# Decode attention: keys and probabilities transposed on VectorE, scores of four heads in one matmul

## The chip, the cores and the metric

One core of one Trainium2 chip runs the whole program. The metric is the device time of one launch in microseconds (us). TensorE is called PE, VectorE DVE, ScalarE ACT, GpSimd POOL and the queue of SyncE SP. A difference under 0.2% (0.4 us) counts here as no difference.

## The reference, cut to what matters

```python
xn = layernorm(x)                                   # x: [8, 1, 512], bf16
q  = (xn @ wq) -> [8 batches, 32 heads, 128]        # wq: [512, 4096]
k, v = caches[:, :, 8192 - 2048:, :]                # [8, 8 kv heads, 2048, 128] are read
s  = einsum(q, repeat(k, 4)) * 128 ** -0.5          # four query heads share one kv head
o  = softmax(s) @ repeat(v, 4)                      # per batch: 32 heads x 128
attn = o.reshape(8, 1, 4096) @ wo                   # wo: [4096, 512]
glu  = (sigmoid(xn @ w_gate) * (xn @ w_up)) @ w_down   # F = 1792
out  = x + attn * silu(glu)
```

With eight rows of x the arithmetic is small. What is large is the data: 64 MiB of keys and values in the window and 13 MiB of weights are read once.

## The kernel before

**Transfers.** All large transfers are issued on SP's queue into nine slots of SBUF (16 KB a partition each). `pump` issues the next transfer of a list in a fixed order as soon as `free` returns a slot. The list is: the gate, up and down weights, the query weights `wq`, then the key tiles and value tiles of the eight batches in turn (a tile is 2 MiB: one batch, four kv heads, 2048 positions), the value tile three places behind the key tile, and last `wo` in four pieces of 16, 10, 4 and 2 rows a partition. The key tiles are numbered k0 to k15 here and the value tiles v0 to v15 (two a batch); k15 is thus followed by v12, v13, v14, v15 and the four pieces of `wo`, wo16, wo10, wo4 and wo2.

`w_down` has 1792 rows, 14 x 128. The first 11 x 128 come as one transfer over all partitions, 11 KB each (`want_down`, `MT = 11`). The rest comes in eight small transfers (`want_side`): four of 5, 5, 3 and 3 partitions with 15 KB each, four of 9 partitions with 4 KB each.

**Per batch.** A key tile has its positions on the partitions and must be turned, since the contraction of the scores is over the 128 values of a head. `k_transposes` does it on PE: 8 transposes of 128x128 into a PSUM tile `kT_ps`, which DVE copies to `kT_sb` (line 461), 16 such steps a batch. `scores` then runs four matmuls a pair of steps, one for each kv head l, side by side in the four column groups of the array, each with 32 columns of weights (line 474); all scores of a batch end in one PSUM bank of 128 rows, where a row is one query head and one quarter of its positions, and the 512 columns are those positions:

```python
nc.tensor.matmul(
    s_ps[b][NR * l : NR * (l + 1), :],
    lhsT=qm_sb[:, b, i * G + l, o : o + Z],
    rhs=t[:, :, PG * l : PG * (l + 1)],
```

`row_max` takes the maximum of each row on DVE (line 487) and four exponentials on ACT (line 494, 32 rows each). The maxima and sums of the rows of one head are brought to one value by `stat_rows`, `factor` and `spread` on one partition. `p_transposes` turns the probabilities on PE (line 563) and DVE copies them to `pT_sb` (line 568). `value` multiplies them with the value tile (line 584): for the batches under `WIDE = 5` one matmul a kv-head group with 64 columns of weights and 512 moving columns, from batch 5 on two with 32 and 256. `combine` (ACT, line 604), `normalise` (PE and DVE, lines 614 and 623) and `turn` (lines 632 and 639) put the batch's outputs into `oP_sb`.

**Order.** Each engine runs in the order in which the program was written; the scheduler is off. In batch b's 16 steps PE also does the softmax work of batch b-1 and the values of batch b-2. After the loop the last two batches are finished, and `fin_ps` takes 32 x 4 matmuls of 128 columns over `wo` (line 706); two DVE operations (lines 717 and 719) and four small output transfers end the program.

## Time and profile before

| | |
|---|---|
| median of 3 runs | 199.16 us (199.14 to 199.21) |
| the profiled execution's own time | 199.33 us |
| its span, first to last instruction | 197.5 us |
| mean granted PE clock | 0.965 |
| read from memory | 81.01 MB |
| PE busy | 157.4 us, 2112 matmuls |
| DVE busy | 125.4 us, 245 instructions |
| ACT busy | 40.7 us |
| POOL busy | 11.0 us |

Busy time is what an engine spent in instructions. Matmuls overlap in the array, so PE's figure is an upper one. 1.83 us of the profiled execution's own time lie outside its span. In the rows of groups, `x128 | 84.2, 683` means 128 instructions, 84.2 us busy, 683 ns each. The time in which an engine was idle before them, and what ended it, stands behind the next bar.

### The profile page before, as it was taken

What the parts mean: (1) busy time and instruction counts of PE and PEld (TensorE: products, weight loads), DVE (VectorE), ACT (ScalarE), POOL (GpSimd) and SP (SyncE); (2) the same over time, 40 slices, a digit from 0 to 9 for tenths busy, and PEclk for the clock granted to TensorE, in tenths of its full rate; (3) what the DMA queues carried; (4) which work ended last, traced back from release to release, by engine and by line L of the source; (5) the groups of instructions that cost most, each with busy time, mean ns of one, the idle gap of its engine ahead of it and who ended that gap; (6) DMA issues with size and microseconds to landing.
All of it is one profiled execution on the core that took longest, in us unless ns stands there. A gap on an engine that the chain in (4) does not pass through costs nothing.

```text
span 197.5 us, 4796 instructions
## 1 busy us (share of the span) xinstructions
PE 157.4 (80%) x2112; PEld 103.1 (52%) x2112; DVE 125.4 (63%) x245; ACT 40.7 (21%) x95; POOL 11.0 (6%) x22
## 2 busy tenths in 40 slices
PE   0089559999788898799979987999799979976733
PEld 0034325776664565466545654566466556655531
DVE  4623106999797696679666965796669658935201
ACT  0522022006306001600160016001600160071000
POOL 8910200000000000000000000000000000000000
PEclk9999859999999999999999999999999999999975
DMA  6999999999999999999999999999999999999980
GB/s 205 424 440 435 431 434 435 425 425 431 423 425 425 438 428 435 431 425 428 422 433 431 435 425 433 428 418 428 428 438 431 428 428 431 428 423 425 428 366 21
DMA packets 6396, 81.32 MB, mean 412 GB/s; under 512 B 812, under 2 KB 820, under 8 KB 1624
## 3 DMA queue, kind: packets, MB, share of 16 engines
q1 hardware_dynamic: 6328, 81.01, 96.6%
q8 instruction: 16, 0.26, 0.5%
q10 hardware_dynamic: 48, 0.01, 0.0%
q14 instruction: 4, 0.03, 0.0%
HBM read 81.01 MB, written 0.01 MB: 410 GB/s over the span
## 4 chain that ended last, share of the span: by engine, by line
DMA 73%; PE 22%; POOL 3%; SPq 0%; issue 0%; DVE 0%; POOLq 0%
DMA v_sb<-in_A_v_cache_dram 46%; DMA wo_sb<-in_A_wo_dram 14%; PE kT_ps L456 11%; DMA wq_sb<-in_A_wq_dram 7%; DMA k_sb<-in_A_k_cache_dram 6%; PE o_ps L584 4%; PE s_ps L474 3%; POOL side L126 2%; PE m_ps L614 1%; PE fin_ps L706 1%; PE pT_ps L563 1%; SPq L131 0%; POOL perm L206 0%; POOL hT_sb L245 0%; DVE prod L717 0%
## 5 line engine op out<-in xcount | busy, mean ns | idle before, releaser
L461 DVE COPY kT_sb<-kT_ps 128x1024 bf16<-128x1024 bf16 x128 | 84.2, 683 | 28.9 <-PE kT_ps L456 25.0
L456 PE MATMUL kT_ps<-perm,k_sb 128*128 128x128 bf16 x1024 | 72.6, 220 | 3.7 <-DMA k_sb<-in_A_k_cache_dram 3.7
L456 PEld LDWEIGHTS <-k_sb 128*128 128x128 bf16 x1024 | 58.8, 98 | 26.1 <-issue 16.8
L584 PE MATMUL o_ps<-v_sb,pT_sb 128*32 128x256 bf16 (+1 forms) x352 | 36.5, 327 | 9.0 <-DMA v_sb<-in_A_v_cache_dram 7.6
L474 PE MATMUL s_ps<-kT_sb,qm_sb 128*32 128x512 bf16 x256 | 25.6, 389 | 1.3 <-DVE kT_sb L461 1.1
L494 ACT ACTIVATE p_buf<-s_ps,st 32x512 bf16<-32x512 f32 x32 | 21.7, 679 | 15.4 <-DVE st L487 15.1
L584 PEld LDWEIGHTS <-pT_sb 128*32 128x32 bf16 (+1 forms) x352 | 12.3, 101 | 21.7 <-issue 19.7
L604 ACT ACTIVATE o_sb<-o_ps,fac 128x512 f32<-128x512 f32 (+1 forms) x8 | 4.9, 608 | 60.9 <-PE o_ps L584 60.9
L568 DVE COPY pT_sb<-pT_ps 128x1024 bf16<-128x1024 bf16 x16 | 10.8, 676 | 1.8 <-PE pT_ps L563 1.8
L474 PEld LDWEIGHTS <-qm_sb 128*32 128x32 bf16 x256 | 7.0, 93 | 8.0 <-issue 1.3
L563 PE MATMUL pT_ps<-turn_rows,p_buf 128*128 128x128 bf16 x128 | 10.7, 227 | 0.0
L563 PEld LDWEIGHTS <-p_buf 128*128 128x128 bf16 x128 | 9.4, 149 | 0.2 <-issue 0.2
L521 ACT ACTIVATE w_row<-w 1x128 f32<-1x128 f32 x8 | 2.5, 309 | 30.6 <-DVE w L514 30.6
L235 PE MATMUL xnT_ps<-ident,xn_bf 8*128 8x8 bf16 x4 | 0.3, 176 | 10.6 <-DVE xn_bf L224 10.6
L385 DVE COPY qm_sb<-qT_ps 128x128 bf16<-128x128 bf16 x2 | 1.4, 881 | 8.7 <-PE qT_ps L380 8.7
L301 DVE TENSOR_TENSOR h_bf<-sig,u_ps 8x448 bf16<-8x448 f32 x4 | 2.4, 608 | 6.6 <-PE u_ps L294 6.1
L278 PE MATMUL g_ps<-wg_sb,xnT_sb 128*8 128x448 bf16 x16 | 5.7, 544 | 0.3 <-DVE xnT_sb L242 0.3
L494 ACT ACTIVATION_READ_ACCUMULATOR p_buf<-s_ps,st 32x1 f32 x32 | 5.9, 184 | 0.0
L706 PE MATMUL fin_ps<-wo_sb,oP_sb 128*32 128x128 bf16 x128 | 3.3, 263 | 3.1 <-DMA wo_sb<-in_A_wo_dram 3.1
L487 DVE TENSOR_REDUCE st<-s_ps 128x1 f32<-128x512 f32 x8 | 5.4, 681 | 0.5 <-PE s_ps L474 0.5
L235 PEld LDWEIGHTS <-xn_bf 8*128 8x128 bf16 x4 | 0.2, 117 | 10.6 <-DVE xn_bf L224 10.6
L352 PE MATMUL q_ps<-wq_sb,xnT_sb 128*32 128x512 bf16 x32 | 3.1, 526 | 3.2 <-DMA wq_sb<-in_A_wq_dram 3.2
(88 smaller groups left out, 92.0 us busy)
## 6 DMA issues: line engine op xcount, KB each, us to landing
k_sb<-in_A_k_cache_dram SPq DMA_DIRECT2D x16, 2048.0 KB
v_sb<-in_A_v_cache_dram SPq DMA_DIRECT2D x16, 2048.0 KB
wq_sb<-in_A_wq_dram SPq DMA_DIRECT2D x2, 2048.0 KB
wo_sb<-in_A_wo_dram SPq DMA_DIRECT2D x1, 2048.0 KB
wg_sb<-in_B_w_gate_dram SPq DMA_DIRECT2D x2, 896.0 KB
wu_sb<-in_B_w_up_dram SPq DMA_DIRECT2D x2, 896.0 KB
wd_sb<-in_B_w_down_dram SPq DMA_DIRECT2D x1, 1408.0 KB
wo_sb<-in_A_wo_dram SPq DMA_DIRECT2D x1, 1280.0 KB
```

The costliest lines, as they stand in the source:

```text
L126: nc.gpsimd.memzero(t[:M_AT])
L278: nc.tensor.matmul(g_ps[:], lhsT=xnT_sb[:, kt, :B], rhs=weights[("wg_sb", kt)][:, k * FC : (k + 1) * FC], start=(kt == 0), stop=(kt == KT ...
L456: nc.tensor.transpose(out=kT_ps[:, c, :], in_=k_sb[:, j * CU + h * CH + c, :], identity=perm[:],)
L461: nc.vector.tensor_copy(out=kT[(b, u)][:, h * CH : (h + 1) * CH, :], in_=kT_ps[:])
L474: nc.tensor.matmul(s_ps[b][NR * l : NR * (l + 1), :], lhsT=qm_sb[:, b, i * G + l, o : o + Z], rhs=t[:, :, PG * l : PG * (l + 1)], start=(u ...
L487: nc.vector.tensor_reduce(out=st[b][:], in_=s_ps[b][:], axis=AX.X, op=ALU.max, negate=True)
L494: nc.scalar.activation(out=p_buf[b % 2][rows, :, l, :], in_=s[rows, :].rearrange("k (c p) -> k p c", p=PG), func=AF.Exp, bias=st[b][rows, ...
L563: nc.tensor.transpose(out=pT_ps[:, c, :], in_=p_buf[b % 2][:, :, :, h * CH + c].rearrange("k p l -> k (p l)"), identity=turn_rows[:],)
L568: nc.vector.tensor_copy(out=pT[b][:, h * CH : (h + 1) * CH, :], in_=pT_ps[:])
L584: nc.tensor.matmul(o_ps[r] if b < WIDE else o_ps[r, 0:2], lhsT=pT[b][:, c, r], rhs=x, start=(c == 0), stop=(c == CU - 1), tile_position=(0 ...
L604: nc.scalar.activation(out=o[:, :n], in_=o_ps[:, :n], func=AF.Copy, scale=fac.pop(b)[:])
L706: nc.tensor.matmul(fin_ps[Z * j : Z * (j + 1), :], lhsT=oP_sb[:, t, :], rhs=weights[("wo_sb", t)][:, j * P : (j + 1) * P], start=(t == 0), ...
```

## The change

Keys are no longer turned by PE. DVE transposes each quarter of a key tile in place, in blocks of 32x32, as 32-bit words: a word is a pair of neighbouring bf16 values, and stays a pair. In a key tile a group of 32 partitions holds 8 positions of each of the four kv heads. After the transpose a partition of the group holds one pair of head dimensions, and the 32 words along it are the group's 8 positions of four heads. The contraction over the 128 values of a head is then four matmuls (two halves of the 64 pairs, two members of a pair), and one matmul over all 128 partitions serves the four groups at once: the query weights are laid out (`widen`, on POOL, four copies a batch) so that a column is nonzero only on its own group's 32 partitions. The moving operand is read with a step of two bf16 values.

A row of the scores is a query head and a group's positions, but its 512 columns hold the positions of all four kv heads. A first matmul (`of_row`, `other`) puts -1e30 into the columns of the three other kv heads, so that their exponentials are zero. A batch has four banks of scores instead of one, so the exponentials are four of 128 rows by 512 rather than four of 32 rows by 512, and the row maximum is taken four times.

The maximum is taken over all rows of a head before the exponentials (`both_max`, `head_max`, with two small PE transposes), so the four parts of a head have the same bias and one sum; `stat_rows` and `spread` go. The probabilities are turned by one DVE transpose of pairs a batch (`p_turn`). All batches use the wide form of `value`.

The steps are 8 a batch instead of 16, the values of batch b-2 lie in its last four. The PSUM pool of the transposes goes and the pool of the scores has six banks. The query projection uses all 128 columns of weights (32 matmuls as before, one after another instead of four at a time). `want_down` brings 13 x 128 rows, 13 KB a partition, and the eight side transfers bring the rest in pieces of 5, 5, 5, 5, 3, 3, 3 and 3 partitions of 4 KB. At the end, the first 16 rows of `wo` are multiplied in 16 matmuls of 512 columns into `f_ps`, copied by ACT, and added to `fin_ps` by `fold` ahead of row 26.

```diff
-    LOW, SF = (5, 5, 3, 3), 15
-    MID, SM = 9, 4
-    MT = 11
+    LOW, SF = (5, 5, 3, 3), 4
+    MT = 13
...
-    def k_transposes(b, u, h):
...
+    def k_turn(b, s):
+        i, j = s // NJ, s % NJ
+        x = (
+            k_tiles[(b, i)][0][:, j * CU : (j + 1) * CU, :]
+            .rearrange("p c d -> p (c d)")
+            .bitcast(f32)
+        )
+        nc.vector.transpose(out=x, in_=x)
+
+    def scores(b, s):
+        i, j = s // NJ, s % NJ
+        if j % 2 == 0:
+            s_ps[(b, s // 2)] = ps_s.tile([P, CU, Z], f32, name="s_ps", tag="s")
+            nc.tensor.matmul(
+                s_ps[(b, s // 2)][:],
+                lhsT=of_row[:].rearrange("k y l r -> k (y l r)"),
+                rhs=other[:],
+                start=True,
+                stop=False,
+            )
+        k = k_tiles[(b, i)][0][:, j * CU : (j + 1) * CU, :].rearrange(
+            "p c (x k e) -> p x e c k", x=2, e=2
+        )
+        for n in range(NE):
+            o = (i * NE + n) * P + M0 - NL * (j % 2)
+            nc.tensor.matmul(
+                s_ps[(b, s // 2)][:],
+                lhsT=q_wide[b % 2][:, o : o + P],
+                rhs=k[:, n // 2, n % 2],
+                start=False,
+                stop=(j % 2 == 1 and n == NE - 1),
+            )
+        if j == NJ - 1:
+            free(k_tiles.pop((b, i)))
...
+    def p_turn(b):
+        pT[b] = ppool.tile([P, NBK, CU // 2, Z, 2], bf16, name="pT_sb")
+        nc.vector.transpose(
+            out=pT[b][:].rearrange("p m c x e -> p (m c x e)").bitcast(f32),
+            in_=p_buf.pop(b)[:].rearrange("k m c x e -> k (m c x e)").bitcast(f32),
+        )
...
+        for s in range(1, NS):
+            tasks[s].append(lambda s=s: scores(b, s - 1))
+        for m in range(NBK - 1):
+            tasks[2 * m + 3].append(lambda m=m: row_max(b, m))
         if b >= 1:
+            tasks[0].append(lambda: scores(b - 1, NS - 1))
+            tasks[0].append(lambda: row_max(b - 1, NBK - 1))
+            tasks[0].append(lambda: both_max(b - 1))
+            tasks[1].append(lambda: head_max(b - 1))
+            tasks[2].append(lambda: exps(b - 1))
+            tasks[6].append(lambda: p_turn(b - 1))
+            tasks[6].append(lambda: factor(b - 1))
+        if b + 1 < B:
+            tasks[3].append(lambda: widen(b + 1))
+        if b >= 2:
+            for s in range(NJ, NS):
+                n = (s - NJ) * NN // NJ
+                tasks[s].append(lambda n=n: values(b - 2, n, n + NN // NJ))
+        if b >= 3:
+            tasks[0].append(lambda: combine(b - 3))
+            tasks[3].append(lambda: normalise(b - 3))
+            tasks[5].append(lambda: turn(b - 3))
+        for s in range(NS):
+            k_turn(b, s)
+            for f in tasks[s]:
+                f()
...
     fin_ps = ps_s.tile([P, P], f32, name="fin_ps", tag="s")
-    for t in range(RT):
+    RG = 16
+    f_ps = ps_s.tile([P, D], f32, name="f_ps", tag="s")
+    for t in range(RG):
...
+    f_sb = ktpool.tile([P, D], f32, name="f_sb", tag="kT")
+    nc.scalar.copy(out=f_sb[:], in_=f_ps[:])
+    for t in range(RG, RT):
+        if t == 26:
+            fold(fin_ps, f_sb, False, False)
```

The instruction lists of the two programs, put side by side, have 4091 entries on PE before and 1504 after, 152 and 175 on DVE, 39 and 28 on ACT, 27 and 37 on POOL.

## Prediction

> **What bounds the kernel now.** I read first the slices of the page, then the batches in the middle, then the end.

> ```profile
> PE 157.4 (80%) x2112; PEld 103.1 (52%) x2112; DVE 125.4 (63%) x245; ACT 40.7 (21%) x95; POOL 11.0 (6%) x22
> PEclk9999859999999999999999999999999999999975
> DMA  6999999999999999999999999999999999999980
> q8 instruction: 16, 0.26, 0.5%
> ```

> The transfers are busy from the second slice to the 38th. The stretch of one batch (start and length, busy time of PE, its weight loads, DVE, ACT and POOL, granted clock, DMA share, GB/s):

> ```profile
> 84.00:103.50 19.50, 17.92 (x222) 11.45 (x220) 14.26 (x29) 4.08 (x10) 0.00 (x0) 1.00 1.01 430
> ```

> Four tiles of 2 MiB at 430 GB/s take 19.5 us. PE needs 17.9 of them, DVE 14.3. No engine decides in the middle; the time is the bytes and the two ends. The end, from the timeline (start, length) and by windows:

> ```profile
> 188.81 1.08 PE L706 MATMUL fin_ps<-wo_sb,oP_sb 128*32 128x128 bf16 x64 [1.12 <-DMA wo_sb<-in_A_wo_dram]
> 191.86 2.28 PE L706 MATMUL fin_ps<-wo_sb,oP_sb 128*32 128x128 bf16 x64 [1.97 <-DMA wo_sb<-in_A_wo_dram]
> 194.19 0.29 DVE L717 TENSOR_TENSOR prod<-gg_sb,fin_ps 128x128 f32<-128x128 f32 x1 [6.16 <-PE fin_ps L706]
> ...
> 190.00:191.50 1.50, 0.00 (x0) 0.00 (x0) 0.00 (x0) 0.00 (x0) 0.00 (x0) 0.59 0.78 321
> 191.50:193.00 1.50, 1.14 (x40) 1.06 (x40) 0.00 (x0) 0.00 (x0) 0.00 (x0) 0.50 0.68 265
> 193.00:194.50 1.50, 1.12 (x31) 0.56 (x23) 0.29 (x1) 0.00 (x0) 0.00 (x0) 0.50 0.02 8
> ```

> PE waits for `wo` twice; its last eight matmuls start at 193.74, 0.38 us after the last packet of `wo` (193.36). So the last transfer sets the end. But the DMA share falls to 0.78 and 0.68 before that: the 16 DMA engines do not end together. I followed the trace's packets engine by engine. A 16 KB packet takes 607 ns (37.9 ns a KB) and the next follows at once; after 3 us an engine pauses only where a packet of a program (q8) comes between, at 0.91 us. Three engines carry all four 15 KB rows and four 4 KB rows of the side transfers, 76 KB; two carry 46 KB, four 16 KB, seven none: a side transfer of n partitions uses the same first n engines. The three heavy ones meet no packet of q8 and end at about 193.0 to 193.37. A light one that meets none ends at 190.1; the rest lie between, by how many of the 16 they got.

> **The change, part by part.**

> *Transfers.* The heavy three carried 11 x 8 + 76 = 164 KB of `w_down`, after the change 13 x 8 + 32 = 136 KB: 28 x 37.9 ns = 1.06 us less. The light ones carry 104 KB for 88, 0.61 us more, 190.7. q8's 16 packets of 16 KB over PE's 4091 entries are 64 bytes an entry, so q8 is PE's program; 1504 entries are 6 packets. A light engine with one ends at 191.6, with two at 192.5. So the last packet comes at about 192.3 for 193.36, and all `wo` and late cache tiles about 1.06 us earlier for the heavy engines.

> *DVE.* The 144 copies of `kT_sb` and `pT_sb` (683 and 676 ns) go, 72 transposes of 128x1024 words come. No row shows one. Two reductions of 32-bit words give the scale: 128 words in 0.271 us (line 510) and 512 in 0.681 (line 487), so 1.068 ns a word and 0.134 fixed. For 1024 words that is 1.23 us. Lower bound 0.67, at which two copies of 1024 elements followed each other; upper bound 2.32, two such steps a word. I take 1.23, since these are the rows on 32-bit data. [...] A batch on DVE is then 9 x 1.23 + 4 x 0.68 (maxima) + 2.2 (nine small operations at 0.14 to 0.29) = 16.0 of 19.5 us.

> *PE.* The 1024 key transposes and 128 of probabilities go. A batch has 32 score matmuls and 4 for the mask, one after another. The nearest row is `u_ps`, 448 columns at 3.19 / 16 = 0.199 us, so 0.228 for 512: 8.2 us. A moving step of two is not in any row; bounds 0.228 and double, I take 0.228 because PE's weight loads from `p_buf` (step 32 bytes) lost only half (149 for 98 ns). Values: 16 pairs at 0.275 (line 584, two concurrent), 4.4. With `normalise` 0.65 and small ones 14.1 us. POOL's `widen` is four copies of 32x128, 0.3 each by line 206's 0.42 for 128x128, hidden: due one batch later.

> *Slots.* A key tile is held until its last scores instead of its last PE transpose, some 2 us longer. At the start the query is late: 16 matmuls one after another, 3.65 for 1.90, then POOL's copies, so first scores near 37 instead of 34.5 us and k0's slot near 40. The transfer that takes this slot is k6, eight tiles (39 us) behind k0: covered by 30 us. Cost nothing; if it were not covered, each us would count.

> *The end.* Here cover is thin. k15 is visible to PE at 164.50, so at 163.44 then. DVE: four key transposes and `p_turn(6)` 6.15, one maximum 0.68, `oP` 0.29, `factor` 0.69, a wait for `turn` 0.3: 171.55. Last scores 0.91, maximum 0.68, then `both_max`, `head_max` and the bias, six steps of 0.14 to 0.27 with PE between, 1.42: 174.56. Exponentials 4 x 0.785 (line 494, start to start): 177.7. `p_turn` 1.23: 178.93, by when the one bank `o_ps` is free too (values of batch 6 on PE to 178.3, `combine` 0.69). Values of batch 7: 32 x 0.228 one after another, since a half has its own columns, `normalise(6)` 0.65, `turn` 0.2: 187.1 (v15 is there at 182.85). `combine` to `oP_sb` took 2.2, now with 512 columns 2.4; with 0.3 for PE's own end it is 189.8. Against 188.08 before. Then 16 wide matmuls 1.33 (four at 0.33, line 474): 191.15; rows 16 to 25 0.68; the copy to `f_sb` 0.59 runs beside them; `fold` 0.43 (line 337) to 192.3, rows 26 to 29 0.27 to 192.6; the last two rows wait for wo2, visible at 192.68, plus 0.45: 193.13 for 194.19, a gain of 1.06. But the cover is 0.1 us, over 30 us of handoffs between three engines. I give 0.4 to handoffs that pass it and take 0.65.

> Sum: 199.33 - 0.65 = 198.68 as a profiled execution. Its own time was 0.17 above the median, so 198.5 for the median. Bounds in this case: 198.1 (cover holds) and 198.75.

> **The rivals.** *PE's clock falls at the end (slower).* In the trace the clock is 0.50 from 190.3 on, after a stretch of 3.4 us in which PE was busy 1.5 (186.9 to 190.3); at 0.50 the last 64 matmuls took 2.28 us, for 1.08 at 1.00. The changed kernel is emptier: PE works 14.1 of 19.5 us, waits about 2 us before each key tile, and is nearly idle for 2.4 us between the last value and `oP_sb`. At 0.50 the last part is 1.90 (16 wide, as `q_ps` took at 0.50) + 1.43 + 0.86 + 0.86 + 0.35 = 5.4 us from 189.8: 195.2, 1.0 later than before, 200.2; had the clock fallen before k15 too, some 0.5 to 1 more. It decides once such a stretch holds less than about half PE work. For: the trace's own fall at 1.5 of 3.4. Against: windows with 2.1 of 3.4 stayed at 1.00 (46.9 to 50.3). [...]

> *Cover lost, nothing gained.* The handoffs cost 0.7 to 1.4 us instead of 0.4, or another engine ends last (two packets of q8 on one, 192.5, or on a heavy one, 193.2): 198.8 to 199.5. For: 32 value matmuls in a row and six small steps hang on one chain.

> *The transpose needs twice as long a word.* Then 9 x 2.32 + 4.9 = 25.8 us a batch on DVE exceed 19.5: 33 before k0, 8 x 25.8 and 25 for the end, about 264 us. From 1.62 us each DVE sets the pace. Against: the two reductions' 1.07 ns a word.

> **How the numbers follow.** Cover case 0.47 (faster), lost cover 0.20 (same), clock 0.28 and slow transpose 0.05 (slower). Under 0.4 us, 0.2%, a measurement of this kernel can't be told from no change. The range 198.0 to 200.6 takes in the first three but for a clock that falls twice; the likeliest case alone is 198.0 to 198.75.

> **What would show it.** Transposes at 1.23 us; DMA share at 1.0 to about 190 and a last `wo` packet near 192.3; q8 with 6 packets; `oP_sb` near 190, PEclk 1.00 in 189 to 193. Wrong: transposes over 1.6 us, PE waiting for DVE while DMA share falls in the middle, `fin_ps` ending over 0.6 us after the last packet, or a PEclk of 0.50 before it.

## The result, and the profile after

| | before | after |
|---|---|---|
| median | 199.2 us (199.09 to 199.29, 11 runs) | 201.16 us (199.67 to 205.88, 11 runs) |
| ratio of after to before | | 1.0082 (1.006 to 1.0105) |
| the profiled execution's own time, its span | 199.33, 197.5 | 199.67, 197.9 |
| mean granted clock of the profiled execution | 0.965 | 0.897 |

The kernel is slower by 0.8%, and its executions lie 6 us apart where those of before lay within 0.2. All ratios here leave out executions that are over 1.5% above the fastest of their kernel; of after's eleven these are three, of 203.56 us and more. The profiled execution of after is the shortest of the eleven: what it shows is the changed kernel at its best, and the other 1.5 us of the median have to be looked for in other executions. First its page (busy time; granted clock and DMA share in 40 slices; the queue of PE's program):

```profile
PE 157.5 (80%) x845; PEld 63.2 (32%) x846; DVE 125.7 (64%) x201; ACT 36.9 (19%) x86; POOL 17.0 (9%) x59
PEclk9999699589997579999955999998599879999999
DMA  6999999999999999999999999999999999999970
q8 instruction: 6, 0.10, 0.2%
```

The DMA share is as full as before, and q8 has its 6 packets. New is the clock: before the change it was at 0.50 from 23.0 to 29.8 us and from 190.3 on, and here it is at 0.50 in six stretches before the end, of 3.4 to 10.2 us each. The groups of the turned keys, their scores and the turned probabilities (count, busy time, mean ns of one):

```profile
L449 DVE STREAM_TRANSPOSE k_sb<-k_sb 128x1024 f32<-128x1024 f32 x64 | 77.4, 1225 | 5.5 <-DMA k_sb<-in_A_k_cache_dram 5.5
L467 PE MATMUL s_ps<-k_sb,q_wide 128*128 128x512 bf16 x256 | 77.3, 433 | 4.5 <-DVE k_sb L449 3.9
L530 DVE STREAM_TRANSPOSE pT_sb<-p_buf 128x1024 f32<-128x1024 f32 x8 | 9.6, 1203 | 0.0
```

A transpose takes 1.225 us. The 433 ns of a score matmul is the time of overlapping ones counted whole; the timelines below show four in 1.03 us. Then the stretch of one batch and the three stretches of the end, as before (PE, its weight loads, DVE, ACT, POOL, clock, DMA share, GB/s), and the end's timeline:

```profile
84.00:103.50 19.50, 17.00 (x85) 6.45 (x85) 15.92 (x24) 6.13 (x17) 1.15 (x4) 0.89 1.01 429
190.00:191.50 1.50, 1.08 (x9) 0.98 (x9) 0.29 (x1) 0.00 (x0) 0.00 (x0) 1.00 0.80 325
191.50:193.00 1.50, 1.11 (x21) 0.58 (x25) 0.30 (x1) 0.00 (x0) 0.00 (x0) 1.00 0.35 135
193.00:194.50 1.50, 1.37 (x76) 1.09 (x68) 0.00 (x0) 0.58 (x1) 0.00 (x0) 1.00 0.00 0
```

```profile
164.15 2.37 DVE L449 STREAM_TRANSPOSE k_sb<-k_sb 128x1024 f32<-128x1024 f32 x2 [1.16 <-DMA k_sb<-in_A_k_cache_dram]
...
176.39 2.78 PE L558 MATMUL o_ps<-v_sb,pT_sb 128*64 128x512 bf16 x24
...
177.20 0.69 ACT L520 ACTIVATE p_buf<-s_ps,bias 128x512 bf16<-128x512 f32 x1
...
179.28 0.69 ACT L582 ACTIVATE o_sb<-o_ps,fac 128x512 f32<-128x512 f32 x1 [1.30 <-PE o_ps L558]
179.33 0.30 DVE L615 CAST oP_sb<-m_ps 128x32 bf16<-128x32 f32 x1 [2.54 <-PE m_ps L608]
179.44 1.25 DVE L530 STREAM_TRANSPOSE pT_sb<-p_buf 128x1024 f32<-128x1024 f32 x1
...
180.74 1.91 PE L558 MATMUL o_ps<-v_sb,pT_sb 128*64 128x512 bf16 x8 [0.61 <-DVE pT_sb L530]
...
182.59 1.08 PE L590 MATMUL m_ps<-ident_f,o_sb 128*128 128x32 f32 x8
...
191.72 0.30 DVE L615 CAST oP_sb<-l_ps 128x32 bf16<-128x32 f32 x1 [0.28 <-PE l_ps L608]
...
192.07 1.05 PE L681 MATMUL f_ps<-wo_sb,oP_sb 128*32 128x512 bf16 x16 [0.39 <-DVE oP_sb L615]
...
194.62 0.29 DVE L707 TENSOR_TENSOR prod<-gg_sb,fin_ps 128x128 f32<-128x128 f32 x1 [2.60 <-PE fin_ps L696]
```

The end no longer waits for `wo` at all. Its last packet is there at 192.94; `f_ps` starts at 192.07 because DVE's last copy to `oP_sb` ends then, and everything behind it waits for that. The chain from k15 (line 449, the first that waits for a DMA) through the last batch has become the bound.

### The profile page after: what moved, and what is told of

It is laid out like the page before. It is cut to its first block, busy times and chain, and to the rows that moved or that the text cites. A ratio compares the mean times of both kernels' runs of the same rounds, so it can differ in the third digit from the quotient of the medians.

```text
span 197.9 us, 2228 instructions
## 1 busy us (share of the span) xinstructions
PE 157.5 (80%) x845; PEld 63.2 (32%) x846; DVE 125.7 (64%) x201; ACT 36.9 (19%) x86; POOL 17.0 (9%) x59
## 4 chain that ended last, share of the span: by engine, by line
DMA 43%; PE 35%; DVE 16%; POOL 2%; ACT 1%; issue 1%; SPq 1%; DVEq 0%; ACTq 0%
DMA k_sb<-in_A_k_cache_dram 31%; PE s_ps L467 15%; PE o_ps L558 12%; DVE k_sb L449 9%; DMA wq_sb<-in_A_wq_dram 7%; DMA wu_sb<-in_B_w_up_dram 5%; DVE st L482 3%; PE s_ps L455 2%; PE m_ps L590 1%; PE q_ps L336 1%; DVE pT_sb L530 1%; POOL qc L367 1%; SPq L99 1%; PE l_ps L590 1%; PE f_ps L681 1%
## 5 line engine op out<-in xcount | busy, mean ns | idle before, releaser
L449 DVE STREAM_TRANSPOSE k_sb<-k_sb 128x1024 f32<-128x1024 f32 x64 | 77.4, 1225 | 5.5 <-DMA k_sb<-in_A_k_cache_dram 5.5
L467 PE MATMUL s_ps<-k_sb,q_wide 128*128 128x512 bf16 x256 | 77.3, 433 | 4.5 <-DVE k_sb L449 3.9
L558 PE MATMUL o_ps<-v_sb,pT_sb 128*64 128x512 bf16 x256 | 38.0, 395 | 0.6 <-DVE pT_sb L530 0.6
L467 PEld LDWEIGHTS <-q_wide 128*128 128x128 bf16 x256 | 22.8, 105 | 39.4 <-issue 24.5
L520 ACT ACTIVATE p_buf<-s_ps,bias 128x512 bf16<-128x512 f32 x32 | 21.5, 686 | 56.4 <-DVE bias L516 56.4
L482 DVE TENSOR_REDUCE st<-s_ps 128x1 f32<-128x512 f32 x32 | 21.4, 669 | 4.6 <-PE s_ps L467 4.4
L558 PEld LDWEIGHTS <-pT_sb 128*64 128x64 bf16 x256 | 13.9, 112 | 18.7 <-issue 9.4
L375 POOL COPY q_wide<-qc 32x128 bf16<-32x128 bf16 x32 | 9.2, 287 | 90.9 <-PE s_ps L467 89.4
L455 PE MATMUL s_ps<-other,of_row 4*128 4x512 bf16 x32 | 14.1, 440 | 2.7 <-POOL of_row L411 2.7
L494 PE MATMUL m_ps<-ident_f,top 128*2 128x128 f32 x8 | 2.4, 296 | 14.3 <-DVE top L491 14.3
L530 DVE STREAM_TRANSPOSE pT_sb<-p_buf 128x1024 f32<-128x1024 f32 x8 | 9.6, 1203 | 0.0
```

Of the source, the lines that this page charges most:

```text
L375: nc.gpsimd.tensor_copy(out=q_wide[b % 2][g, : NW * P].rearrange("p (x c) -> p x c", x=NW)[:, :, M0 + Z * a : M0 + Z * a + NL], in_=qc[g, ...
L449: nc.vector.transpose(out=x, in_=x)
L455: nc.tensor.matmul(s_ps[(b, s // 2)][:], lhsT=of_row[:].rearrange("k y l r -> k (y l r)"), rhs=other[:], start=True, stop=False,)
L467: nc.tensor.matmul(s_ps[(b, s // 2)][:], lhsT=q_wide[b % 2][:, o : o + P], rhs=k[:, n // 2, n % 2], start=False, stop=(j % 2 == 1 and n == ...
L482: nc.vector.tensor_reduce(out=st[b][:, m // 2, m % 2 : m % 2 + 1], in_=s_ps[(b, m)][:].rearrange("k c x -> k (c x)"), axis=AX.X, op=ALU.max,)
L520: nc.scalar.activation(out=p_buf[b][:, m], in_=s_ps.pop((b, m))[:].rearrange("k (c e) x -> k c x e", e=2), func=AF.Exp, bias=bias[:, m // ...
```

## The experiments

The median of before on the chips of the experiments was 199.17, 199.23, 199.22, 199.2 and 199.09 us in the five sets of runs; each ratio is against the runs beside it.

**after_again**: the changed kernel once more, for a second profile.

> The changed kernel once more, for a second profile. Theory 1 (PE's clock): the changed kernel leaves PE idle for some 2 us before each key tile, the granted clock drops to 0.50 for stretches whose place differs from execution to execution, and where such a stretch lies after 150 us the last batch ends later: 199.7 to 206, and the profile has an oP_sb copy of the last batch later than 192.0 if a 0.50 stretch lies between 150 and 195 us. Theory 2 (the chain alone): the last batch's chain of handoffs is late by a fixed 0.4 to 2 us, with all stages stretched alike, whatever the clock shows. Theory 3 (memory): the spread comes from slower transfers; then the last wo packet lies later than 193 in a slow profile.

200.4 us (199.22 to 203.23, 10 runs), ratio 1.0057 (1.0023 to 1.0091). Its profile is of an execution of 203.23 us, the kind that the first profile lacked. Batch 7's scores over k14 and what follows:

```profile
158.30 1.89 PE L467 MATMUL s_ps<-k_sb,q_wide 128*128 128x512 bf16 x4
...
160.66 1.89 PE L467 MATMUL s_ps<-k_sb,q_wide 128*128 128x512 bf16 x4
...
163.91 1.89 PE L467 MATMUL s_ps<-k_sb,q_wide 128*128 128x512 bf16 x4
...
170.21 1.03 PE L467 MATMUL s_ps<-k_sb,q_wide 128*128 128x512 bf16 x4
170.40 0.30 DVE L615 CAST oP_sb<-m_ps 128x32 bf16<-128x32 f32 x1 [3.10 <-PE m_ps L608]
...
173.21 1.23 DVE L449 STREAM_TRANSPOSE k_sb<-k_sb 128x1024 f32<-128x1024 f32 x1
...
194.50 0.30 DVE L615 CAST oP_sb<-l_ps 128x32 bf16<-128x32 f32 x1 [0.28 <-PE l_ps L608]
...
194.85 1.16 PE L681 MATMUL f_ps<-wo_sb,oP_sb 128*32 128x512 bf16 x16 [0.39 <-DVE oP_sb L615]
...
198.18 0.29 DVE L707 TENSOR_TENSOR prod<-gg_sb,fin_ps 128x128 f32<-128x128 f32 x1 [3.39 <-PE fin_ps L696]
```

The clock was 0.50 from 158.1 to 168.4, so four score matmuls took 1.89 us instead of 1.03. The last two key transposes stand on DVE behind the copy of 170.40, and that copy waited 3.10 us for the late PE (0.53 in after). The last key transpose ended at 174.44 for 171.66, and the last copy to `oP_sb` started 2.78 us later. The clock fell again at 195.7, and from the start of `f_ps` to `prod` it took 3.33 us for 2.55: together the 3.56 us by which `prod` is later. The last packet of `wo` came at 193.64, long before it was needed.

**warm**: six 512-column matmuls that feed nothing, at the start and in the middle of each batch.

```diff
+            if s == NJ:
+                keep_warm(b, s // 2)
...
+            tasks[0].append(lambda: keep_warm(b, 0))
```

> Six extra matmuls of 512 columns twice a batch, in the places where PE otherwise waits for a key tile; results overwritten by the mask matmul. Theory 1: granted clock 0.95 or more, spread of the runs under 0.6 us, median 199.5 to 200.0 (what is left is the fixed late end of 0.4). Theory 2 and 3: median near 201 and the same spread, since 2.6 us more PE work a batch helps neither a chain nor memory.

200.34 us (199.31 to 203.62, 5 runs), ratio 1.0064 (1.0044 to 1.0084): a miss. The mean clock rose only to 0.937 to 0.964, and an execution of 203.62 was among the five. The profiled one (199.31) had no fall between 128.4 and 196.6, and so no group of 1.89 in batch 7; even then `prod` started at 194.24.

**early**: `p_turn(last)` stands ahead of `turn(last - 2)`, so that DVE turns the last probabilities before it waits for PE's values.

```diff
-    turn(last - 2)
     combine(last - 1)
     p_turn(last)
+    turn(last - 2)
```

> Only the order of the last batch: p_turn stands ahead of turn of batch 5 in DVE's order. In the profile of the changed kernel p_turn starts at 179.44 though the exponentials end at 177.97, behind the copy of turn. Theory 2: p_turn starts at 178.1, the values of batch 7 then wait for combine (179.97) and start 0.7 us earlier; the time falls by 0.7 in each run. Theory 1: the same 0.7 on the median, spread unchanged.

199.92 us (198.60 to 203.28, 10 runs), ratio 1.0014 (0.9992 to 1.0035). The shortest is 0.6 below after_again's. That is what the timeline of after allows: `p_turn` stood 1.5 us late, but `combine` gave the bank `o_ps` back only at 179.97, so the values of batch 7 (180.74) could start 0.7 earlier and no more. The long executions stay. In its profile (203.17) the clock was 0.50 in 156.7 to 163.6 and 177.2 to 180.6, and the 24 value matmuls took 4.08 us for 2.78.

**narrow**: batch 7 alone in the form of the kernel before (32 columns of weights, 256 moving, two halves of a value tile side by side; `normalise` with two selections instead of four).

```diff
+    WIDE = 7
...
+        if b < WIDE:
+            parts = [(slice(h * i, h * (i + 1)), w, v, o_ps[b][h * i : h * (i + 1)])]
+        else:
+            parts = []
+            for j in range(2):
+                r = slice(h * i + Z * j, h * i + Z * (j + 1))
+                parts.append((r, w[:, Z * j : Z * (j + 1)], v[:, j], o_ps[b][r, 0:2]))
```

> Batch 7 alone multiplies its values as the kernel before did from batch 5 on: matmuls with 32 columns of weights and 256 moving columns, so two run at a time inside a half. Values of batch 7: 7.3 us become 3.9; combine and normalise 0.6 less. Theory 2: the end is then set by the last wo packet (192.3 to 192.9) and not by the chain, profile 1.0 us faster than the changed kernel, 198.6 to 198.9. Theory 1: the same in an execution with full clock, and about 3 us of cover for the others: median 198.8 to 199.6 with a few still late.

198.85 us (198.64 to 199.80, 10 runs), ratio 0.9988 (0.9977 to 1.0). The mean clock of the profile, 0.870, is lower than after's, and yet none of the ten executions is over 199.80: the chain ends (`oP_sb` at 187.32) 5.6 us before the last packet of `wo` (192.90). In this profile no score group of batch 7 was slow; that a fall of the clock ahead of k14 and k15 now has room is seen in narrow_early and narrow_oldside (table below).

**narrow_early**: both.

> Batch 7 with the values and the outputs in the form of before (32 columns of weights, 256 moving), and p_turn of batch 7 ahead of turn(5). If the length of the last batch's chain is what lets a low clock reach the end (theory 1), each of the two takes 1 to 2 us out of the chain, and both together leave it ahead of wo in every execution: oP_sb by 187, the end set by wo alone, median 198.6 to 198.9, all executions within 0.5 us of each other (narrow alone had 198.64 to 199.80). If the clock sets the end by itself (theory 2: the last matmuls over wo at 0.50), nothing is gained over narrow: 198.85, with the same spread up to 199.8.

198.68 us (198.54 to 198.89, 7 runs), ratio 0.9974 (0.9964 to 0.9985). Its end waits for `wo` again, twice, as before the change, and at a clock of 0.50 from 187.6:

```profile
187.19 0.30 DVE L635 CAST oP_sb<-l_ps 128x32 bf16<-128x32 f32 x1 [0.28 <-PE l_ps L628]
...
188.25 1.90 PE L701 MATMUL f_ps<-wo_sb,oP_sb 128*32 128x512 bf16 x16 [1.09 <-DMA wo_sb<-in_A_wo_dram]
...
191.29 1.26 PE L716 MATMUL fin_ps<-wo_sb,oP_sb 128*32 128x128 bf16 x40 [1.14 <-DMA wo_sb<-in_A_wo_dram]
...
193.67 0.29 DVE L727 TENSOR_TENSOR prod<-gg_sb,fin_ps 128x128 f32<-128x128 f32 x1 [6.17 <-PE fin_ps L716]
```

**narrow_hot**: narrow_early with four idle matmuls ahead of `f_ps` and eight behind it.

> narrow_early with twelve matmuls of 512 columns more that feed nothing: four ahead of f_ps, eight behind it, in PE's waits for wo16 and wo10. With the chain short, what stands behind wo10's arrival is 72 matmuls; at a clock of 0.50 they took 2.37 us in narrow (191.42 to 193.79), at 1.00 they would take about 1.5 by after's profile (0.68 + 0.43 + 0.41). If the clock answers to what PE did in the last few us (theory 2), it stays at 1.00 to 193 here, prod starts at about 193.3 (held by the last packet of wo at 192.9 + 0.4), median 198.3 to 198.5. If the fall of the clock at 190 does not come from the idle PE, the fillers run at 0.50, end near 192 and the median is 198.9 to 199.6.

199.0 us (198.51 to 208.49, 12 runs), ratio 0.9996 (0.9977 to 1.0015). The clock did stay at 1.00 to 198.1, and the part behind the last idle matmul took 1.34 us (192.60 to 193.94) for 2.38 in narrow_early. But in the profiled execution k14's scores had been slow, `oP_sb` came at 189.02, and then the fillers themselves held up `f_ps` and the rows behind it. What the clock gave, they took. But for the fillers the chain is as short as in narrow_early, and still four of the twelve executions lie at 199.62 and above; they are the four with the lowest mean clocks (0.851 to 0.871). None of them was profiled, the one of 208.49 neither.

**narrow_oldside**: narrow_early with the side transfers of the kernel before.

> narrow_early with w_down's transfers as before the change (11 x 128 rows, side pieces of 15 KB and 4 KB). The forecast put 1.06 us of last packet on the new pieces; the profile of after showed only 0.42 (192.94 for 193.36). If the pieces are worth what was forecast, and the end follows wo, the last packet comes at 193.4 or later and the median is 0.5 to 1.0 above narrow_early, about 199.4 to 199.8. If the time of the last packet is set by which engine met PE's program packets and by the turn-round of the slots, the difference is under 0.3: 198.7 to 199.1.

199.1 us (198.94 to 199.79, 11 runs), 0.42 above narrow_early; the last packet of `wo` at 193.19 for 192.78. Neither forecast is met: the pieces are worth 0.4, not 1.06 and not nothing.

**spread**: the values of batch b-2 over steps 1 to 7, one half tile after the other.

> The changed kernel with the values of batch b-2 over steps 1 to 7 (first half tile in steps 1 to 3, second in 4 to 7) instead of both in steps 4 to 7. PE then works about 17 of 19.5 us a batch instead of 14, with natural work and no wait over about 1.5 us; the last batch's chain is as long as in after. If the low clock in the middle and at k15 comes from the idle stretches ahead of each key tile (theory 2), the mean clock goes from 0.88 to 0.95 or more and the executions draw together near after's lowest, 199.2 to 200.0, without those of 201 and above. If the chain alone makes the spread (theory 1), or the clock falls at random, the clock stays near 0.88 and the times at 199.2 to 203, median about 200.4.

211.7 us (211.48 to 212.22, 4 runs). Half the expectation holds: the mean clock rose from about 0.89 to 0.934 to 0.943. But a value matmul that does not run beside another costs its full time: in after's end timeline eight of one half took 1.91 us, 0.24 each, and 24 of both halves 2.78, 0.12 each. PE was busy 18.33 us of the stretch 84.0 to 103.5, and in batch 7 no key tile was waited for any more. PE had become the bound: it holds 60% of the chain that ended last, for 35% in after.

**hold**: twelve idle matmuls in batches 6 and 7 alone, nine in the wait for the first key tile, three ahead of its first scores.

> The changed kernel with 12 matmuls of 512 columns that feed nothing in batches 6 and 7 alone: nine while PE waits for the batch's first key tile (some 2.2 us), three ahead of its first scores. In the profiles so far the executions differ by how many of batch 7's first score groups took 1.89 us (clock 0.50) instead of 1.03: with two of them the last key transpose ended at 171.7 and the last oP copy started at 191.7, with three and more at 172.9 to 174.4 and 193.9 to 194.5. If that is the cause of the spread (theory 2, the clock ahead of k15), no group of batch 7 takes 1.89 here, the last key transpose ends at 171.2 to 171.8 in every execution, and the times lie at 199.2 to 199.9, median about 199.4, none above 200.5. If executions over 200.5 come at the same rate as in after_again (4 of 10), or the profiled one is late with a clock of 1.00 in 150 to 172, something other than the clock makes the spread.

```profile
153.80:157.20 3.40, 1.21 (x6) 0.38 (x5) 2.89 (x4) 0.19 (x1) 0.00 (x0) 1.00 1.00 429
```

```profile
154.70:158.10 3.40, 1.55 (x6) 0.48 (x6) 3.33 (x7) 0.00 (x0) 0.00 (x0) 1.00 1.03 441
```

```profile
154.00:157.40 3.40, 2.72 (x13) 1.06 (x12) 2.71 (x4) 0.00 (x0) 0.00 (x0) 1.00 1.02 429
```

With 1.21 and 1.55 us of PE work the clock fell at the stretch's end, with 2.72 it did not. What hold had instead were late transfers: k15 at 164.47, the last packet of `wo` at 193.60.

**before_newside**: the kernel before with nothing but the new side transfers.

> The kernel before with nothing but the new side transfers (13 x 128 rows of w_down and eight pieces of 4 KB a partition). narrow_oldside against narrow_early put these at 0.42 us, and the forecast at 1.06. The kernel before ends with the last packet of wo (193.36, prod at 194.19), so it should gain what the last packet gains: 0.3 to 0.5 us by the experiment (198.7 to 198.9), 1.06 by the forecast (198.1), and nothing (199.2) if PE's 16 program packets, which this kernel keeps, end on the engines that the pieces have relieved.

199.97 us (199.62 to 201.49, 12 runs), ratio 1.0051 (1.0033 to 1.007): slower, against all three expectations. The last packet of `wo` came at 194.24. What differs in its trace are the 16 KB packets themselves. They follow each other after 607 ns, but between 16 and 28 us many took 681 to 722, and single ones up to 995. The two stretches (24 to 28 us) of before_newside and of narrow_oldside show the same DMA share and different GB/s:

```profile
24.00:28.00 4.00, 1.09 (x12) 0.49 (x15) 0.00 (x0) 0.00 (x0) 0.00 (x0) 0.50 0.98 361
```

```profile
24.00:28.00 4.00, 2.78 (x14) 1.18 (x13) 0.00 (x0) 0.00 (x0) 0.00 (x0) 1.00 1.00 423
```

I summed what the packets over 640 ns took above 607 between 16 and 30 us, and divided the sum by the 16 engines: 0.89 us in before_newside, 1.08 in after_again, 1.27 in early, 0.98 in hold, 0.31 to 0.38 in after, warm, narrow, narrow_early and narrow_hot, 0.01 or less in before and narrow_oldside. In before_newside this mean is as large as the delay of the last packet (194.24 for 193.36). That it is the whole reason is not shown: the three heavy engines carry 1.06 us less, which should have brought the last packet forward, and whether PE's 16 program packets took that back was not followed. (The expectations that follow give such means up to 40 us.)

**after_oldside** and **hold_oldside**: the changed kernel, and hold, with the side transfers of before.

> The changed kernel with w_down's transfers as before the change. Reading the 16 KB packets one by one showed something new: with the new pieces they take up to 720 ns instead of 607 between 16 and 28 us, until the next group of small pieces; summed over 16 engines this is 0.37 us in the profile of after, 0.38 to 0.41 in warm and narrow, 1.00 in hold, 1.12 in after_again, 1.30 in early, 0.91 in before_newside, and 0.03 to 0.05 in before and narrow_oldside. Theory 3 (the new pieces leave the engines in step and their packets slow, in some executions longer than in others): here the sum is under 0.1 us, k15 comes at 163.6 to 164.0 each time, and most executions lie at 199.3 to 199.8, median 199.5, below after's 200.4, although the three heavy engines are back. Theory 2 (the clock alone): the spread stays, 199.2 to 203, median 200.4 or more.

> Both suspects taken away from the changed kernel: w_down's transfers as before, and twelve matmuls that feed nothing in batches 6 and 7 as in hold. If the late executions come from the two together (low clock at k14 and k15, slow packets at 16 to 28 us), these executions lie within 0.5 us of each other, at 199.2 to 199.7, with k15 at 163.6 to 164.0 and prod 30.5 us behind it. If a third cause is left, executions above 200.3 remain.

202.27 us (200.61 to 205.90, 6 runs) and 201.2 us (199.99 to 202.71, 6 runs). Both miss what theory 3 expected of them: the packets' mean fell to 0.19 and 0.01, and the times rose. So the slow packets do not make the long executions. hold_oldside's profile (200.13) has no slow group, k15 at 164.59 and `prod` at 195.06, 30.47 us later. With the old side transfers k15 is late in narrow_oldside too (164.56, for 163.90 in narrow_early, one profile each), and where the end hangs on k15 it follows. Executions above 200.3 remain, four of six, so a third cause beside those two suspects is not excluded. Its six executions lie nearly in the order of their mean clocks: 199.99 and 200.13 at 0.929, 201.17 and 201.24 at 0.923, 202.71 at 0.897, 202.48 at 0.880. after_oldside's profile (205.90) has the clock at 0.50 twice, from 136.3 to 150.0 and from 160.2 to 170.5, three groups of 1.89 in batch 7, and `prod` at 200.74.

**narrow_flat**: narrow_early with `w_down` in one transfer of 14 KB a partition, and no side transfers.

```diff
-    LOW, SF = (5, 5, 3, 3), 4
-    MT = 13
+    MT = 14
...
-    for x in sides[:2]:
-        want_side(B_w_down, *x)
```

> narrow_early with w_down in one transfer of 14 KB a partition, no side transfers at all: all engines carry 112 KB of it, for 136 on the heavy three and 104 on the light ones. By balance alone the heavy engines end 0.9 us earlier, the last packet of wo comes near 191.9 instead of 192.78, and the median is 198.0 to 198.3. By theory 3 the engines' phases decide: if they run in step here from the start, packets of 681 to 720 ns appear and stay for long, since nothing breaks the step, and the median is 199 or far above (each us of packet time summed over the engines counts).

199.36 us (198.91 to 202.47, 12 runs), ratio 1.0014 (0.9998 to 1.0031). No packet between 16 and 30 us was slow (0.00), although by the transfers' sizes all engines carry the same bytes (112 KB of `w_down` each); equal loads are thus not what makes packets slow. The last packet came at 192.25 and `prod` started at 193.09, 0.58 before narrow_early's. But the span ended at 197.7, 4.6 us behind `prod` instead of 3.3:

```profile
193.09 0.29 DVE L675 TENSOR_TENSOR prod<-gg_sb,fin_ps 128x128 f32<-128x128 f32 x1 [6.19 <-PE fin_ps L664]
...
193.73 1.12 SPq L679 DMA_DIRECT2D out_dram<-y_bf  x2
```

SP's output issues took 1.12 us for 0.68, and a program packet of 8 KB that came at 167.5 in narrow_early came at 195.47. Its chain is short too, and yet four of its twelve executions lie above 200 us (200.03 to 202.47), at mean clocks of 0.835 to 0.859; none was profiled.

**narrow_flat2**: the same with `w_down`, `wq` and the four pieces of `wo` each issued in two halves, seven issues more on SP.

> narrow_flat with seven more DMA issues on SP's queue (w_down, wq and the four pieces of wo each in two halves). In narrow_flat the last packet of wo came at 192.25 (192.78 in narrow_early) and prod started at 193.09 (193.67), but the span ended 4.6 us behind prod instead of 3.2: a program packet of 8 KB at 195.47, which in narrow_early came at 167.5, and output issues of 1.12 us instead of 0.68. SP's program there is eight DMA issues shorter. If it is the program's packet, which sits where the program's length puts it, then here the packet is back before 170, the end 3.2 us behind prod, and the median is 198.0 to 198.4, better than narrow_early's 198.68. If the 1.4 us come from something else in one transfer of w_down, the median stays near 199.4.

198.41 us (198.30 to 198.59, 5 runs), ratio 0.9963 (0.9949 to 0.9977), the best median of all, though its interval and narrow_early's overlap. The packet came at 172.1, and the issues are back at 0.72:

```profile
193.19 0.29 DVE L676 TENSOR_TENSOR prod<-gg_sb,fin_ps 128x128 f32<-128x128 f32 x1 [5.91 <-PE fin_ps L665]
...
193.83 0.72 SPq L680 DMA_DIRECT2D out_dram<-y_bf  x2
```

**The profiles side by side** (of the kernels that turn the keys on DVE, without spread). The columns: durations of batch 7's slow score groups (four score matmuls, 1.03 at full clock), end of the last key transpose, start of the last copy to `oP_sb`, last packet of `wo`, start of `prod`, all in us.

| profile | slow groups | keys end | oP_sb | last wo | prod |
|---|---|---|---|---|---|
| warm | none | 171.18 | 191.35 | 192.84 | 194.24 |
| hold | none | 171.98 | 192.11 | 193.60 | 195.00 |
| hold_oldside | none | 172.10 | 192.16 | 193.41 | 195.06 |
| after | 1.56, 1.89 | 171.66 | 191.72 | 192.94 | 194.62 |
| after_again | 1.89, 1.89, 1.89 | 174.44 | 194.50 | 193.64 | 198.18 |
| after_oldside | 1.19, 1.89, 1.89, 1.89 | 176.77 | 196.84 | 193.33 | 200.74 |
| early | 1.89, 1.89, 1.81 | 172.90 | 193.90 | 193.82 | 198.12 |
| narrow | none | 171.36 | 187.32 | 192.90 | 193.79 |
| narrow_early | 1.66, 1.89 | 171.40 | 187.19 | 192.78 | 193.67 |
| narrow_oldside | 1.89, 1.89, 1.69 | 172.64 | 187.92 | 193.19 | 194.01 |
| narrow_hot | 1.22, 1.89, 1.89, 1.89 | 173.74 | 189.02 | 192.83 | 193.94 |
| narrow_flat | 1.79, 1.83 | 170.96 | 186.60 | 192.25 | 193.09 |
| narrow_flat2 | 1.89, 1.89, 1.59 | 171.71 | 186.98 | 192.51 | 193.19 |

In the wide form, in the order of after, `oP_sb` comes 20.1 to 20.2 us after the last key transpose whatever the clock did before, and with two slow groups or fewer `prod` starts 30.5 us behind k15 (30.57 in warm, 30.53 in hold, 30.47 in after and in hold_oldside). It ends behind `wo` every time. In the narrow form the same slow groups are there, and `wo` ends last: in narrow_oldside the keys ended 1.0 us later than in after, in an execution of 199.08. (In narrow_hot the fillers ended last.)

## Why the prediction was wrong, point by point

**Right.** The transpose: 1.225 us for 1.23, and DVE with 15.92 us a batch for 16.0. A word thus took 1.2 ns, fixed part included, in line with the 1.07 ns of the reductions, and the upper bound of 2.32 us is excluded. The moving operand's step of two costs nothing that shows: four score matmuls took 1.03 us, and four idle ones of narrow_hot, whose moving columns lie side by side, 1.02. The forecast's 0.91 for four was taken from another matmul and was low either way. q8's 6 packets, the slots, and the middle that the transfers bound, came out as written.

**The step that failed is the end's chain, and with it the cover.** The forecast was a profiled execution of 198.68 us and a median of 198.5; the shortest execution took 199.67 and the median was 201.16. Forecast and profile of after: key transposes end 171.55 and 171.66; bias 174.56 and 175.10; `p_turn` ends 178.93 and 180.69; values end 187.1 and 189.20; `oP_sb` 189.8 and 192.02. Of these last 2.2 us, 1.5 came in at one handoff: `p_turn` was put at the exponentials' end (177.89), but it stands on DVE behind the copy of `turn(5)`, and that waits for 24 value matmuls on PE (176.39 to 179.17), so it started at 179.44. The forecast had looked at what `p_turn` needs and not at what is queued ahead of it. The bank of the values was mis-timed with it: forecast free at 178.99 (178.3 and 0.69), it was free at 179.97. So another place of `p_turn` alone gives 0.7 back and not 1.5; narrow_early against narrow shows it, with `p_turn` 1.39 earlier and the values 0.64. That the key transposes ended only 0.1 late is luck: k15 was there 0.7 later than forecast (164.15 for 163.44), and what stands between its arrival and their end took 0.6 less. The bias was 0.4 later beyond the 0.1 of the key transposes, the four exponentials 0.35 quicker, and `normalise(6)` took 1.08 for 0.65: 0.65 was the narrow form's, with half the selections. From `oP_sb` to `prod` it took 2.60 us for the forecast's 3.33, so `prod` came 1.5 later than forecast (194.62 for 193.13). The cover of 0.1 us behind which `wo` was to end was in truth minus 0.85 (194.62, against 192.94 plus the 0.83 that `prod` followed the last packet by before).

**The last packet was over-sized.** It was forecast at 1.06 us earlier, by bytes alone; after showed 0.42, narrow_oldside against narrow_early 0.41, and on the kernel before the same pieces made it 0.88 later. The sum by bytes took 607 ns a packet as given, and with the new pieces many take longer between 16 and 28 us: 0.34 us an engine in after, about half of the 0.64 that is missing.

**The clock rival was right in kind, and sized for the wrong place.** It was written for the last matmuls (200.2), with "some 0.5 to 1 more" had the clock fallen before k15. In after's profile the last part ran at 1.00. What the three long executions that were profiled have is a fall ahead of k14's and k15's scores. By the ends of the key transposes against 171.66 they are 2.8 us late in after_again and 5.1 in after_oldside; of the 5.1, 2.6 were there when k14's first transpose started (156.88 for 154.28), behind the fall of 136.3 to 150.0 in batch 6. The forecast also had PE emptier than it was: in after it worked 17.0 of 19.5 us a batch at full clock too (110.0 to 129.5), for 14.1. That the clock falls when a stretch of 3.4 us holds less than about half PE work held in kind (fell at 1.21 and 1.55, stayed at 2.72). The stretch of before that the forecast set against it, 46.9 to 50.3, holds 2.2 us by the trace, not 2.1. Over the sixteen profiles (PE's work by the modelled ends of its matmuls) every such stretch at 1.00 with under 1.77 us of PE work was followed by 0.50 (66 of them) and none with over 2.42; of the 107 between, 39 were and 68 were not. An idle stretch is not needed for a fall: in after PE worked over a third of the one ahead of 157.2 (1.21 of 3.40). The falls at 157.2, 158.1, 160.2 and 156.9 in four profiles of nearly the same program (after, after_again, after_oldside, narrow_early; the first two are one program, 0.9 us apart) lie in different places, which would make one program's executions differ.

Both rivals thus came together: cover lost, which puts the kernel at 199.3 to 200.4 where batch 7 has no slow group or two (profiles of warm, after, hold_oldside and hold), and the clock, which comes on top in the long executions that were profiled. Shown: that the chain ends last and costs the gain (with it shortened, narrow_early waits for `wo` again and is 0.26% faster than before), and that slow groups in batch 7 come with late ends, which after_again's timeline follows from handoff to handoff. Not settled is how much of the longer executions is the clock's. Idle matmuls in the waits (warm, hold) did not lower the median, and warm has an execution of 203.62 at a mean clock of 0.949. Long executions were profiled only in after_again, early and after_oldside. For the others there is the mean clock alone, and it goes with the time in hold_oldside, narrow_hot and narrow_flat, but not in after_again (199.22 at 0.877, 203.23 at 0.890).

## What to carry to other kernels

When a step is taken off the bound, add up the chain at the end in each engine's own program order, with what is queued ahead of every link; a cover of 0.1 us over 30 us of handoffs is no cover. An emptier engine may run slower: in these profiles a wait ahead of a key tile that left PE under half busy for 3.4 us often halved its clock (always under 1.77 us of work), for the next 3.4 to 13.7 us, which shows only where no transfer hides it. And a part that looks independent, here the side transfers, is worth its own run: it was worth -0.42 us in one kernel and +0.75 in another, depending on what stood around it.

## What the runs showed that was not expected

- With the eight 4 KB-row pieces, 16 KB packets of 681 to 722 ns instead of 607 stood between 16 and 28 us (as a mean of 16 engines, what they took above 607 came to 0.31 to 1.27 us); with 15 KB and 4 KB rows there were hardly any (0.00 to 0.19), with no pieces none (0.00, narrow_flat). Why is open; equal loads on all engines do not bring it about (narrow_flat).
- A program packet of 8 KB at 195.47 us came with 1.3 us more behind `prod`; seven more DMA issues on SP moved it to 172.1 and the 1.3 us were gone. How the packet costs them is not shown: SP's issues were slow from 193.73 on, before it started.
- In after_again the clock stayed at 0.50 from 158.1 for three stretches of 3.4 us in which PE was busy throughout, in after from 157.2 for one. Over the sixteen profiles 80 such full stretches at 0.50 were followed by 1.00 and 32 by 0.50 again, and no stretch with under 2.5 us of work brought the clock back. What tells them apart was not tried.
